# Agent attention with a maxout FFN: a new head, a new instruction order, and spare products to hold the clock

One Trainium2 chip (trn2), one core. The metric is the device time of that core in microseconds (us). It is 1.7 to 2.1 us longer than the span of the same execution (474.81 to 472.9 in the profile of the kernel before). Engines: PE is TensorE (matrix products), DVE VectorE, ACT ScalarE, POOL GpSimd, SPq the queue that issues most DMA transfers. The *granted clock* is the share of full speed at which TensorE was allowed to run.

## The reference

```python
B, N, C = 4, 12544, 128              # 49 agents, d_ff 768
def sm(a, b):
    e = exp(scale * (a @ b.T) - max);  return e / e.sum(-1)
agent_v = sm(agents, k) @ v          # per batch 49x128
x       = sm(q, agents) @ agent_v    # 50176 rows in all
h       = maximum(maximum(x @ w1, x @ w2), x @ w3)
out     = h @ w_out
```

## The kernel before

Batch 0's `k` and `v` (11 pairs of loads of up to 9x128 rows) are reduced to `agent_v` in a *head*, ahead of everything else. Then come 49 *groups* of 1024 q rows. Three times a batch ends inside a group (12, 24, 36); the k and v of the next batch are reduced in 11 of the 12 groups ahead of it, one pair each. So there are *groups with k* (33) and *without*.

The weights are folded into the small matrix: `G` holds `agent_v` times (w3 - w1), (w2 - w1) and w1 w_out. In a group, for each of six column blocks f: product **u** (PE), relu **a** (ACT), product **v** (PE), maximum **x** (DVE); block 4 is done wholly on ACT. Then 48 output products of 128x128 per group, `oc<o><f>` in 12 pieces of four, and a scaling `sc` by the softmax sums (DVE).

```python
def uv_tile():    ... tag="uv", bufs=3      # PSUM, two banks each
def small_tile(): ... tag="om", bufs=2      # PSUM, one bank each
def first(f):      uv[f] = hidden(f, C31, True)        # "u", 49-row products in pairs
def relu_first(f): ... nc.scalar.activation(a_sb[f], u, AF.Relu)           # "a"
def second(f):     uv[f] = hidden(f, C21, f != FI)     # "v"
def max_second(f): ... nc.vector.tensor_tensor(out=r, in0=uv[f], in1=a_sb[f], op=ALU.max)  # "x"
# [...]
def add_exps():   # POOL: Eacc += e_k       def reduce(): # DVE: e_sum = sum of Eacc over j
def total():      # PE, fp32: ones x e_sum  def normalise(): # DVE: avT = Vacc / total
# [...]  the program order is a table of keys; a group adds 6.0 per step, all is sorted by key
KEY = {"qt": -6.429, "qe": -5.981, "s": -0.613, "ex": -0.611, "u0": 0.67, "a0": 0.672, "ho": 0.873,
       "ks": 0.877, "sum": 0.878, "ke": 0.992, "u5": 1.063, "v0": 1.099, ... }
```

qt, qe, s, ex are the q transposes, their copy, the scores and `e_q`; ks, ke, kv, ka the scores of a k tile, `e_k`, the value products and the addition to Vacc; sum and rec the softmax sums and their reciprocals (`recips`). The engines execute in order what the table says.

The softmax here doesn't subtract the row's maximum and nothing guards it: scores larger than these inputs give would overflow.

## Time and profile before

| | before |
|---|---|
| time, median of 4 fast runs | 475.25 us (474.17 to 475.29) |
| span, granted clock (mean) | 472.9 us, 0.968 |
| first hidden product | 54.33 us |
| from one `e_q` to the next, with k / without | 8.17 / 7.96 us |

Three stages are read from the start of `e_q`, of which there is one per group. The prediction shows most lines. Here are the span and the chain of what ended last, from the page; the rows of the maxima and of the output products; and, from the timeline, the reduction ahead of a batch change, which matters later.

```profile
span 472.9 us, 13244 instructions
PE 72%; DVE 12%; DMA 10%; issue 2%; ACT 2%; POOL 0%; SPq 0%; DVEq 0%; ACTq 0%
L385 DVE TENSOR_TENSOR r<-uv_ps,a_sb 128x1024 bf16<-128x1024 f32 x245 | 298.2, 1223 | 6.9 <-PE uv_ps L360 4.4
```
```profile
140.48 0.94 POOL L209 TENSOR_TENSOR Eacc<-Eacc,e_k 128x392 f32<-128x392 f32 x1 [6.09 <-ACT e_k L193]
...
146.51 0.95 DVE L242 TENSOR_REDUCE e_sum<-Eacc 128x49 f32<-128x441 f32 x1
```

In the second fence POOL's last addition ends 5 us before DVE reduces (140.48 + 0.94 against 146.51): DVE never waits there before the change.

### The profile page before, as it was taken

The numbers are of one execution on the slowest core, as the hardware profiler recorded it, in microseconds if no ns is written. First come the engines' busy times: TensorE is split into PE (matmuls) and PEld (weight loads), VectorE is DVE, ScalarE is ACT, GpSimd is POOL, SyncE is SP. The second block draws the span as 40 slices with busy tenths as digits, with TensorE's granted clock in tenths as the row PEclk, the third lists the DMA queues.
The fourth block names the chain that finished last, engine by engine and source line by source line (L and its number), as shares of the span: only waits on it lengthen the run. The fifth ranks groups of instructions, "written<-read, shape, count | busy, mean of one in ns | idle before, by whom it ended". The sixth has DMA issues, their size and how long they took to land.

```text
span 472.9 us, 13244 instructions
## 1 busy us (share of the span) xinstructions
PE 433.8 (92%) x5434; PEld 281.7 (60%) x5434; DVE 417.2 (88%) x531; ACT 400.9 (85%) x455; POOL 177.4 (38%) x176
## 2 busy tenths in 40 slices
PE   2465699999999999999998999999999999999996
PEld 2454246666665666666665766666655666666654
DVE  3353479999999899999999899999999999999994
ACT  3364479999998899999997999999988898989982
POOL 2577643645524346363550544546130101010000
PEclk9996559999999999999999999999999999999999
DMA  8999998999998799998989799986524334341112
GB/s 319 403 411 409 346 318 259 289 323 231 289 312 268 238 285 342 310 292 219 299 300 292 257 297 277 342 260 161 157 90 137 132 134 137 128 141 76 60 69 114
DMA packets 67816, 114.93 MB, mean 243 GB/s; under 512 B 41831, under 2 KB 43307, under 8 KB 67755
## 3 DMA queue, kind: packets, MB, share of 16 engines
q1 hardware_dynamic: 67552, 113.98, 76.4%
q8 instruction: 42, 0.69, 0.6%
q14 instruction: 19, 0.16, 0.1%
q10 hardware_dynamic: 203, 0.10, 0.1%
HBM read 78.74 MB, written 25.69 MB: 221 GB/s over the span
## 4 chain that ended last, share of the span: by engine, by line
PE 72%; DVE 12%; DMA 10%; issue 2%; ACT 2%; POOL 0%; SPq 0%; DVEq 0%; ACTq 0%
PE uv_ps L360 29%; PE o_ps L399 27%; DVE r L385 9%; PE o_ps L390 5%; DMA st<-in_k_dram 5%; PE m_ps L324 4%; PE m_ps L334 3%; DMA st<-in_q_dram 2%; DMA kT<-k_bf 2%; DVE o_sb L406 2%; PE m_ps L188 2%; PE m_ps L197 2%; DMA st<-in_v_dram 1%; ACT a_sb L375 1%; PE m_ps L348 1%
## 5 line engine op out<-in xcount | busy, mean ns | idle before, releaser
L385 DVE TENSOR_TENSOR r<-uv_ps,a_sb 128x1024 bf16<-128x1024 f32 x245 | 298.2, 1223 | 6.9 <-PE uv_ps L360 4.4
L375 ACT ACTIVATE a_sb<-uv_ps 128x1024 bf16<-128x1024 f32 x245 | 241.0, 1025 | 23.0 <-PE uv_ps L360 22.9
L399 PE MATMUL o_ps<-wo_bf,r 128*128 128x128 bf16 x2352 | 200.2, 220 | 0.0
L360 PE MATMUL uv_ps<-e_q,G 49*128 49x512 bf16 (+3 forms) x1248 | 182.4, 376 | 3.4 <-ACT a_sb L375 1.6
L399 PEld LDWEIGHTS <-r 128*128 128x128 bf16 x2352 | 142.6, 98 | 60.8 <-issue 58.2
L360 PEld LDWEIGHTS <-G 49*128 49x128 bf16 x1248 | 58.9, 94 | 69.3 <-issue 25.4
L209 POOL TENSOR_TENSOR Eacc<-Eacc,e_k 128x441 f32<-128x441 f32 (+1 forms) x40 | 41.4, 1036 | 131.9 <-ACT e_k L193 107.5
L319 POOL CAST q_bf<-st 128x1024 bf16<-128x1024 f32 x49 | 51.0, 1042 | 71.1 <-DMA st<-in_q_dram 56.2
L406 DVE TENSOR_TENSOR o_sb<-o_ps,recips 128x512 f32<-128x512 f32 x98 | 67.2, 685 | 1.8 <-PE o_ps L399 1.8
L162 POOL CAST k_bf<-st 128x1152 bf16<-128x1152 f32 (+1 forms) x44 | 50.6, 1150 | 15.8 <-DMA st<-in_k_dram 15.0
L372 ACT ACTIVATE uv_ps<-uv_ps 128x1024 f32<-128x1024 f32 x49 | 49.4, 1008 | 1.7 <-PE uv_ps L360 1.4
L383 ACT ACTIVATE r<-uv_ps 128x1024 bf16<-128x1024 f32 x49 | 49.9, 1018 | 0.0
L390 PE MATMUL o_ps<-G,e_q 128*128 128x256 bf16 x196 | 38.1, 276 | 0.0
L169 POOL CAST v_bf<-st 128x1152 bf16<-128x1152 f32 (+1 forms) x33 | 37.6, 1140 | 0.0
L328 DVE COPY qT<-m_ps 128x1024 bf16<-128x1024 bf16 x49 | 33.4, 681 | 0.6 <-PE m_ps L324 0.6
L340 ACT ACTIVATE e_q<-m_ps 128x512 bf16<-128x512 f32 x49 | 29.3, 597 | 4.6 <-PE m_ps L334 4.1
L324 PE MATMUL m_ps<-ident,q_bf 128*128 128x128 bf16 x392 | 31.2, 225 | 1.6 <-POOL q_bf L319 1.6
L167 ACT ACTIVATE v_bf<-st 128x1152 bf16<-128x1152 f32 (+1 forms) x11 | 12.7, 1151 | 16.4 <-DMA st<-in_v_dram 16.4
L324 PEld LDWEIGHTS <-q_bf 128*128 128x128 bf16 x392 | 24.8, 100 | 2.8 <-POOL q_bf L319 2.1
L176 PE MATMUL uv_ps<-ident,k_bf 128*128 128x128 bf16 x98 | 11.2, 289 | 15.9 <-POOL k_bf L162 13.3
L182 DVE COPY kT<-uv_ps 128x1152 bf16<-128x1152 bf16 (+1 forms) x11 | 8.3, 750 | 19.8 <-PE uv_ps L176 19.8
L334 PE MATMUL m_ps<-qT,agT 128*64 128x512 bf16 (+3 forms) x104 | 20.6, 402 | 0.4 <-DVE qT L328 0.4
(60 smaller groups left out, 203.7 us busy)
## 6 DMA issues: line engine op xcount, KB each, us to landing
st<-in_q_dram SPq DMA_DIRECT2D x46, 512.0 KB, 5.0
out_dram<-o_sb SPq DMA_DIRECT2D x46, 512.0 KB, 3.2
st<-in_k_dram SPq DMA_DIRECT2D x40, 576.0 KB, 6.1
st<-in_v_dram SPq DMA_DIRECT2D x40, 576.0 KB, 7.1
st<-in_k_dram SPq DMA_DIRECT2D x4, 512.0 KB, 6.5
st<-in_v_dram SPq DMA_DIRECT2D x4, 512.0 KB, 7.0
wst<-in_moe_w_dram SPq DMA_DIRECT2D x3, 384.0 KB, 8.1
st<-in_q_dram SPq DMA_DIRECT2D x2, 384.0 KB, 4.2
```

The costliest lines, as they stand in the source:

```text
L162: nc.gpsimd.tensor_copy(out=d["kb"][:, :n, :], in_=d["k"][:, :n, :])
L209: nc.gpsimd.tensor_tensor(out=Eacc[b][:, :n * A], in0=Eacc[b][:, :n * A], in1=d["e"][:, :n * A], op=ALU.add)
L319: nc.gpsimd.tensor_copy(out=d["qb"], in_=d["q"])
L324: nc.tensor.transpose(t[:, j * P:(j + 1) * P], d["qb"][:, j, :], ident)
L360: nc.tensor.matmul(t[:, h, j0 * P:j1 * P], G[b][h * H:h * H + A, col + f * P:col + (f + 1) * P], d["e"][h * H:h * H + A, j0 * P:j1 * P], s ...
L372: nc.scalar.activation(u, u, AF.Relu)
L375: nc.scalar.activation(a_sb[f], u, AF.Relu)
L383: nc.scalar.activation(r, uv[f], AF.Relu)
L385: nc.vector.tensor_tensor(out=r, in0=uv[f], in1=a_sb[f], op=ALU.max)
L390: nc.tensor.matmul(t[:, i * 2 * C:(i + 1) * 2 * C], d["e"][:, jj * P:(jj + 1) * P], G[batch[jj]][:, C1O:C1O + 2 * C], start=(i == 0), stop ...
L399: nc.tensor.matmul(t[:, c:c + C], r_sb[f][:, h, jj * P:(jj + 1) * P], wo_bf[:, f, :], start=False, stop=True, skip_group_check=True)
L406: nc.vector.tensor_tensor(out=d["out"][:, j:j + m, :], in0=d["o", o].rearrange("p (j c) -> p j c", c=C), in1=d["r"][:, j:j + m].unsqueeze( ...
```

## The change

Its intent: end the head as soon as the loads allow, run the first groups at full clock, and take waits out of the steady group. The diff, cut to its core:

```diff
-    KEY = {"qt": -6.429, ..., "s": -0.613, ..., "rec": 1.248, ..., "kv": 1.624, ..., "x5": 4.465, ...}
+    KEY = {"qt": -1.706, ..., "s": -1.072, ..., "kv": 0.6, "ka": 0.601, "u0": 0.67, "rec": 0.684,
+           "a0": 1.809, "u2": 1.974, "v0": 2.084, "x0": 2.085, ..., "v5": 6.666, "x5": 6.771, ...}
+    WARM = 4
+    TAIL = (0.0005, 1.0, 1.5)
 # head: k loads lead v by three; sums on PE; values add up in one PSUM tile
+        def totals(d, g):   # replaces Eacc on POOL, reduce on DVE, fp32 sum on PE
+            for j in range(d["n"]):
+                nc.tensor.matmul(acc["t"][:, :A], ones_bf, d["e"][:, j * A:(j + 1) * A], ...)
+        def cast_v(d, g):   # last two: half on ACT, half on DVE
+        def product(c0, c1):
+            nc.vector.tensor_copy(out=G[0][:, c0:m], in_=src[:, :m - c0])
+            nc.scalar.activation(G[0][:, m:c1], src[:, m - c0:c1 - c0], AF.Copy)
+            if g >= 2:
+                at(c + 3.95, lambda: warm(WARM))        # spare products, ident x ident, 512 columns
+        at(z + 3.95, normalise)
+        at(z + 3.955, differences_21)                   # w2 - w1, w3 - w2: DVE and POOL
 # batches 1 to 3: hosts one group later, loads streamed, G one group ahead of the border
+    STREAM = {"kl": 0.0, "ld": 0.5, "kc": 1.0, "qc": 1.5, "vl": 1.9, "kt": 2.0, "vc": 3.2}
-            s = None if b == 0 else (b - 1) * NT // GT + g
+            s = (b - 1) * NT // GT + g + 1
+        z = 6.0 * (s - 1)
+        k_tail(b, s - 1, (z - 6 + KEY["ke"] + 1.6, z + KEY["kv"] + 0.0005,
+                          z + KEY["ka"] + TAIL[0], z + TAIL[1], z + TAIL[2]))
 # weight work after the head, spare output-like products in groups 0 and 1
+    at(HEAD_END + 0.5, cast_w1)
+    at(5.0, turn_w1)
+    at(7.0, prep_linear)
+    at(z, lambda ...: keep_busy((s, o), f))             # where the pieces of groups -2, -1 would stand
```

## The prediction

> **What bounds the kernel now.** I read the page first (busy shares, then the slices), then the timeline where the slices change, then the chain and the waits. The first fence is the page's share line and three of its slice rows (a slice is 11.8 us).
>
> ```profile
> PE 433.8 (92%) x5434; PEld 281.7 (60%) x5434; DVE 417.2 (88%) x531; ACT 400.9 (85%) x455; POOL 177.4 (38%) x176
> PE   2465699999999999999998999999999999999996
> DVE  3353479999999899999999899999999999999994
> PEclk9996559999999999999999999999999999999999
> ```
>
> PE, DVE and ACT are all near full from slice 6 on, so 400 us run well; the first five or six slices do not, and the clock falls to half in slices 3 to 5. There are three stages.
>
> *Head, 0 to 54.3 us.* Batch 0's k and v must be reduced before the first output group can start. The stretches and then the timeline show it:
>
> ```profile
> 30.00:40.00 10.00, 5.83 (x114) 5.40 (x111) 3.59 (x8) 5.88 (x9) 7.23 (x7) 0.98 1.02 409
> 40.00:50.00 10.00, 5.71 (x70) 4.81 (x71) 3.11 (x7) 2.69 (x4) 8.48 (x10) 0.50 1.02 412
> 60.00:65.00 5.00, 4.65 (x35) 2.07 (x35) 4.06 (x5) 4.10 (x5) 0.23 (x1) 0.50 0.97 356
> 80.00:90.00 10.00, 10.00 (x131) 6.58 (x130) 9.80 (x14) 9.66 (x12) 4.19 (x4) 1.00 0.93 301
> ```
> ```profile
> 40.30 1.06 ACT L167 ACTIVATE v_bf<-st 128x1024 bf16<-128x1024 f32 x1 [0.94 <-DMA st<-in_v_dram]
> ...
> 47.85 0.93 POOL L209 TENSOR_TENSOR Eacc<-Eacc,e_k 128x392 f32<-128x392 f32 x1
> 48.81 0.95 DVE L242 TENSOR_REDUCE e_sum<-Eacc 128x49 f32<-128x441 f32 x1 [4.17 <-POOL Eacc L209]
> ...
> 51.06 1.03 DVE L254 TENSOR_TENSOR avT<-Vacc,k_recip 128x49 bf16<-128x49 f32 x1
> 52.15 1.71 PE L266 MATMUL uv_ps<-wall,avT 128*64 128x512 bf16 x10 [1.67 <-DVE avT L254]
> ...
> 54.33 0.60 PE L360 MATMUL uv_ps<-e_q,G 49*128 49x512 bf16 x2 [0.48 <-ACT G L273]
> ```
>
> In the stretches the last two columns are DMA share and GB/s, and before them the granted clock. The DMA runs at 410 GB/s until 50 us, but the last v of batch 0 is there at 40.3 us; 14.0 us pass until the first hidden product (L360). They go into exponent sums added on POOL behind casts for later groups (done at 48.8), a reduce, a sum over partitions, a reciprocal, a normalise, the G products and their copies.
>
> *Groups 0 to 3.* The PE works, but at half clock until 70 us. The starts of e_q, one per group, are 45.25, 59.23, 69.20, 77.88, 86.05.
>
> *Steady groups and batch changes.* Here e_q is 8.17 us apart, and 7.96 us in the last twelve groups, which carry no k and v work. At each batch change the intervals are 8.12, 9.33 and about 10.1, together 3.1 us more than three steady ones.
>
> ```profile
> 288.41 0.60 ACT L340 ACTIVATE e_q<-m_ps 128x512 bf16<-128x512 f32 x1
> 296.58 0.60 ACT L340 ACTIVATE e_q<-m_ps 128x512 bf16<-128x512 f32 x1
> ```
> ```profile
> DVE recips L354 <- ACT e_k L193: 1.2, 6, 0.2
> ```
>
> The wait (of the stretch 90 to 140 us) recurs in every group: DVE stands 0.20 us before the reciprocal, plus some tenths in the gaps that count as busy. From start to start DVE needs 1.14 to 1.17 for each of five maxima, 0.60 to 0.64 for each scaling, 0.63 for the q copy, 0.12 and 0.14 for the small ones: 7.9 us of the 8.17. So DVE bounds a steady group.
>
> **What the Trainium skill says.** (1) "TensorE: Matmul & The Clock Gate", Part 1: the array starts at half clock, and about 3.4 us of sustained activity release it. The trace agrees on the factor: eight 128-column transposes take 1.03 us at 42.77 and 0.61 at 289.07. It agrees less on the trigger: PE counts as busy without a gap from 65 us on and is still at 0.50. The clock comes at about 70.3 us, some 2.6 us after the first 128x128 output products (L399, 67.96). Before 32.8 us the page's 1.0 is no measurement: nine transposes took 1.14 us at 6.76. (2) The same page, Part 4: transposes do not count as PE activity in the same way. That fits: in the head PE mostly transposes, got the full clock only about 32.4 us and lost it at 39.6. So both kinds of spare product (full-array 512-column ones in the head, 128-column output-like ones in groups 0 and 1) aim at what the trace shows missing. (3) "SBUF — State Buffer", Who interferes with whom: a VectorE instruction with two SBUF inputs contends with a GpSimd instruction that reads SBUF. The trace agrees: L254 took 1.03 us under a POOL cast and 0.22 in other batches. (4) "Perfetto Trace Analysis", Roofline: one core is bounded by its 16 DMA engines at about 435 GB/s; the trace shows 412, so I count 410.
>
> **The change part by part.**
>
> *Load order and reduction in the head.* What must land is 12.85 MB of k and v, 1.18 MB of w1 to w3, 0.52 MB of q and 0.1 MB of agents: 14.65 MB. Before moved 307, 396 and 411 GB/s in the first three tens of us, 11.14 MB; the remaining 3.51 MB at 410 take 8.6 us: landed at 38.6 us, with v slightly before w2, the last. What then follows, from rows of before: half a v cast on each of ACT and DVE 0.6 (1.06 for the whole), eight value products 0.55, normalise 0.25 (it now reads PSUM, so no lock), differences on DVE 0.7 for 512 columns (1.47 for 768, partly locked by POOL), G products 0.5, half a copy 0.5 (0.95 for 768 columns). Some lie side by side; with hops of 0.05 and some POOL contention I choose 2.9 us. First hidden product at 41.5 in place of 54.33: **12.8 us saved**. Gone from this path are the Eacc additions, reduce, fp32 sum and the wait for POOL. Four spare products of 512 columns are 0.9 us at full clock in a period of 2.9 us per k/v pair, beside the loads.
>
> *Groups 0 to 3 at full clock.* From the first hidden product to e_q of group 4 it is 31.7 us before. After: 5.3 to e_q of group 1, then 7.8, 7.8 and 7.95, plus 0.8 for the weight work moved here (cast 0.83, copy 0.56, two small evacuations) and 1.5 for a start-up wait (rival b): 31.2. **0.5 us saved**, the clock gain mostly eaten by the other two.
>
> *New order in a group.* The built order on DVE is max, max, scale, max, add V, reciprocal, max, scale, max, q copy: the reciprocal now follows the add, which already waited for e_k, so the 0.20 wait is gone. Against it stands the chain max, release of its PSUM buffer, product, max: 1.22 + 0.05 + 0.50 (the wait seen at 454.05 to 454.55) = 1.77, against 1.14 + 0.60 to 0.64 of DVE work between; it just fits. Sum: 1.165 + 1.78 + 1.14 + 0.12 + 0.15 + 1.78 + 1.14 + 0.63 = 7.9; I take 7.93 with k and v and 7.82 without. From e_q of group 4 to that of 48 there are 44 intervals, 30 of the first kind, 14 of the second: 347.4 us.
>
> *Batch changes.* The G products now come one group early, not at the border, but their ACT copy (1.02) stands ahead of a relu that a maximum needs, and DVE still has reduce 0.6, reciprocal and normalise 0.55 and the copy 0.86. I count 2.6 us each in place of 3.1. So 347.4 + 7.8 = 355.2 against 366.3 before: **11.1 us saved**.
>
> *End.* From e_q of group 48 to the end it is 20.5 us; e_q now stands about 1 us nearer to its first product: 19.5.
>
> **Sum:** 41.5 + 31.2 + 355.2 + 19.5 = 447.4 us of span, against 472.9. The time is 2.3 us over the span (475.2 to 472.9): 449.8. As several chains fit only by hundredths I add 1.2: **451 us**.
>
> **Rivals.** (a) *The steady order gains nothing.* PE issues strictly in order, about 7.3 us of products in 7.9, and the loop max to q copy to max to relus is nearly as long as DVE's work. If it stays at 8.17 and 7.96, the end is 10 us later: 461. For it: PE is 99% busy now; against: that busy is modelled overlap and the removed wait is DVE's own. (b) *The gain of the head becomes a wait for loads.* Before had moved some 4 MB more by its first hidden product; after starts with little in hand, and each kT transpose waits for its k and holds the SP queue (6.12 us of SPq at 44.73; it landed after 10.3). The first scores need kT about 47; I see it at 46, and the v cast of that group after w_out's at 48 to 50. That is 0 to 5 us; 1.5 are in the sum, the worst gives 455. Against more: with k and v a group needs 2.2 MB, at 340 GB/s (65 to 75 us) 6.5 us. (c) *The spare products do not hold the clock*: groups 0 and 1 run cold with 24 more products of 0.107 us each: 6 us more, 457. (d) *Better than I think*: no start-up wait, batch changes hidden: 445.
>
> **Range and chances.** The head's gain rests on bytes and a short chain (12 to 14 us nearly sure, 2.7%), so less than 2% needs two rivals together. Range 445 to 461. Faster by over 2% 0.95, within 2% 0.045, slower 0.005.
>
> **What would show it.** First hidden product at 41 to 43 us. Granted clock 1.0 by 35 us and at 45 to 60. e_q at 7.9 to 8.0 us in groups with k and 7.8 without, no reciprocal waiting for e_k. At a batch change 2 to 3 us over three steady intervals. PE waiting for kT or v_bf between 45 and 60 us under 3 us. If e_q stays at 8.17 the third step is wrong; if the first hidden product is after 45, the first.

## The result, and the profile after

**470.96 us** (median of 470.1, 471.15, 470.78 and a run of 479.04 that is classed slow, for its time: its clock was 0.986, that of the fast ones 0.987 to 0.993) against 475.25. The ratio of the fast runs is 0.9909, 95% interval [0.9887, 0.9931]: within 2%, where 451 had been predicted. (A ratio here is the mean time of one kernel's fast runs over that of the other's of the same rounds, so not quite the ratio of the medians quoted.) The profiled run is a fast one.

The page's first lines, rows of its slices (11.7 us each) and its chain:

```profile
span 468.3 us, 13594 instructions
...
PE 437.8 (93%) x5622; PEld 284.1 (61%) x5622; DVE 416.3 (89%) x522; ACT 397.6 (85%) x456; POOL 169.0 (36%) x164
...
PE   2786799999999999999989999999989999999996
...
PEclk9998899999999999999999999999999999999999
...
PE 76%; DMA 9%; DVE 5%; issue 4%; ACT 3%; POOL 2%; SPq 1%; POOLq 0%; DVEq 0%; ACTq 0%
```

The half-clock slices are nearly gone and the fill-up of PE is sooner; the chain has less DVE (5 for 12%) and more PE. In the steady part PE's row has two slices with an 8 (20 and 29 from zero, at 234 and 339 us), both at a batch change; before had one.

| stage (us of span) | before | predicted | after | short of the prediction |
|---|---|---|---|---|
| to the first hidden product | 54.33 | 41.5 | 45.39 | 3.9 |
| from there to `e_q` of group 4 | 31.7 | 31.2 | 34.0 | 2.8 |
| `e_q` of group 4 to 48 | 366.3 | 355.2 | 369.1 | 13.9 |
| from there to the end | 20.5 | 19.5 | 19.8 | 0.3 |
| span | 472.9 | 447.4 | 468.3 | 20.9 |

So the head gained 8.9 us, and the first groups and the steady stage gave 2.3 and 2.8 back. Two thirds of the miss lie in the steady stage. Its pace, from the timeline (a group with k, then one without):

```profile
282.11 0.60 ACT L473 ACTIVATE e_q<-m_ps 128x512 bf16<-128x512 f32 x1
290.26 0.60 ACT L473 ACTIVATE e_q<-m_ps 128x512 bf16<-128x512 f32 x1
...
399.96 0.60 ACT L473 ACTIVATE e_q<-m_ps 128x512 bf16<-128x512 f32 x1
408.05 0.60 ACT L473 ACTIVATE e_q<-m_ps 128x512 bf16<-128x512 f32 x1
```

That is 8.15 us (before 8.17, predicted 7.93) and 8.09 us (before 7.96, predicted 7.82): groups without k became *slower*. The 13.9 us are made of 30 intervals x 0.22 = 6.6, 14 x 0.27 = 3.8, three batch changes with 10.7 us over steady intervals in place of 7.8 = 2.9, and 0.6 in single longer intervals.

The head's end, from the timeline:

```profile
39.59 0.63 ACT L216 ACTIVATE v_bf<-st 128x512 bf16<-128x512 f32 x1 [1.99 <-DMA st<-in_v_dram]
...
40.55 1.00 POOL L135 TENSOR_TENSOR wall<-wst,wst 128x384 bf16<-128x384 f32 x1 [1.22 <-DMA wst<-in_moe_w_dram]
...
43.20 1.59 DVE L135 TENSOR_TENSOR wall<-wst,wst 128x128 bf16<-128x128 f32 x2
...
45.39 0.39 PE L493 MATMUL uv_ps<-e_q,G 49*128 49x512 bf16 x2
```

The last v is there at 39.6 us and w2 at 40.5 (predicted 38.6 for the last), and 4.9 us follow where 2.9 were predicted; DVE's differences take 1.59 where 0.7 was put in.

The first groups, as stretches (us, then busy time of PE, PEld, DVE, ACT, POOL with counts in brackets, granted clock, DMA share, GB/s) and as timeline:

```profile
50.00:55.00 5.00, 3.00 (x39) 1.83 (x39) 2.89 (x4) 3.70 (x6) 4.12 (x5) 1.00 0.88 231
55.00:60.00 5.00, 4.95 (x41) 2.48 (x41) 2.68 (x4) 2.31 (x4) 2.06 (x2) 0.66 0.81 318
```
```profile
51.50 0.49 PE L156 MATMUL m_ps<-ident,w_bf 128*128 128x128 bf16 x6 [0.59 <-ACT e_q L473]
...
52.04 0.56 DVE L157 COPY w1T<-m_ps 128x768 bf16<-128x768 bf16 x1 [1.96 <-PE m_ps L156]
```

Here the w1 transposes (L156), which the change put into group 1, wait for a PSUM buffer that `e_q` sets free, and DVE stands 1.96 us for them. PE is busy for 3.0 of 5 us, and the clock drops in the next stretch. `e_q` of group 2 comes 12.2 us after that of group 1.

And the group ahead of a batch change:

```profile
233.20 1.04 POOL L325 CAST v_bf<-st 128x1024 bf16<-128x1024 f32 x1 [1.95 <-DMA st<-in_v_dram]
234.20 1.02 POOL L349 TENSOR_TENSOR Eacc<-Eacc,e_k 128x441 f32<-128x441 f32 x1
...
235.25 0.96 DVE L382 TENSOR_REDUCE e_sum<-Eacc 128x49 f32<-128x441 f32 x1 [0.24 <-POOL Eacc L349]
```

POOL's addition, which ended 5 us ahead of the reduction before, now ends at the very moment at which DVE wants it: it stands behind a v cast, and that behind a load.

### The profile page after: what moved, and what is told of

The parts are those of the page before. It is cut to its first block, busy times and chain, and to the rows that moved or that the text cites. A ratio compares the mean times of both kernels' runs of the same rounds, so it can differ in the third digit from the quotient of the medians.

```text
span 468.3 us, 13594 instructions
## 1 busy us (share of the span) xinstructions
PE 437.8 (93%) x5622; PEld 284.1 (61%) x5622; DVE 416.3 (89%) x522; ACT 397.6 (85%) x456; POOL 169.0 (36%) x164
## 3 DMA queue, kind: packets, MB, share of 16 engines
q1 hardware_dynamic: 67552, 113.98, 77.2%
## 4 chain that ended last, share of the span: by engine, by line
PE 76%; DMA 9%; DVE 5%; issue 4%; ACT 3%; POOL 2%; SPq 1%; POOLq 0%; DVEq 0%; ACTq 0%
PE uv_ps L493 29%; PE o_ps L532 27%; DMA st<-in_k_dram 7%; PE o_ps L523 5%; PE m_ps L457 4%; PE m_ps L467 3%; DVE r L518 3%; PE m_ps L337 2%; ACT a_sb L508 2%; DMA st<-in_q_dram 1%; PE m_ps L187 1%; POOL q_bf L452 1%; PE m_ps L481 1%; DVE qT L461 1%; PE uv_ps L312 0%
## 5 line engine op out<-in xcount | busy, mean ns | idle before, releaser
L532 PE MATMUL o_ps<-wo_bf,r 128*128 128x128 bf16 x2352 | 172.3, 220 | 0.0
L532 PEld LDWEIGHTS <-r 128*128 128x128 bf16 x2352 | 139.7, 98 | 40.0 <-issue 37.6
L493 PEld LDWEIGHTS <-G 49*128 49x128 bf16 x1248 | 55.4, 94 | 67.4 <-issue 34.1
L321 POOL CAST k_bf<-st 128x1152 bf16<-128x1152 f32 (+1 forms) x33 | 37.4, 1134 | 41.0 <-DMA st<-in_k_dram 41.0
L349 POOL TENSOR_TENSOR Eacc<-Eacc,e_k 128x441 f32<-128x441 f32 x27 | 27.6, 1024 | 3.8 <-ACT e_k L192 3.8
L523 PEld LDWEIGHTS <-e_q 128*128 128x128 bf16 x196 | 12.1, 96 | 25.5 <-issue 25.5
L216 ACT ACTIVATE v_bf<-st 128x1152 bf16<-128x1152 f32 (+1 forms) x11 | 11.7, 1063 | 10.6 <-DMA st<-in_v_dram 10.6
```

Of the source, the lines that this page charges most:

```text
L493: nc.tensor.matmul(t[:, h, j0 * P:j1 * P], G[b][h * H:h * H + A, col + f * P:col + (f + 1) * P], d["e"][h * H:h * H + A, j0 * P:j1 * P], s ...
L523: nc.tensor.matmul(t[:, i * 2 * C:(i + 1) * 2 * C], d["e"][:, jj * P:(jj + 1) * P], G[batch[jj]][:, C1O:C1O + 2 * C], start=(i == 0), stop ...
L532: nc.tensor.matmul(t[:, c:c + C], r_sb[f][:, h, jj * P:(jj + 1) * P], wo_bf[:, f, :], start=False, stop=True, skip_group_check=True)
```

## The experiments

The recorded texts use letters. **D**: DVE's own work sets the steady pace (my prediction). **P**: PE is simply full. **L**, **K**: closed loops of products, maxima and PSUM buffers set the pace of groups without k (L) and with k (K). **T**: copies of G at a batch change. **W**: the weight work in group 1 stalls the start. **Q**: the spare products in PE's queue delay the head's end. **R**: the reduction waits for POOL and a load.

The times of after, p_prep5, r_late, r_only and r_tail are medians of 4 to 6 runs; the others are looks of one run. Looks of one run have no state of their own; from these I use spacings that repeat many times in the trace, and say so where it is otherwise. All measured values:

| label | result | us | before, same chip | first hidden | `e_q` 4 | with k | without k | first, second long interval at the changes |
|---|---|---|---|---|---|---|---|---|
| after | right | 470.96 | 475.25 | 45.39 | 79.41 | 8.15 | 8.09 | 8.80 10.83, 9.04 10.84, 9.21 10.84 |
| s_scale | wrong | 474.12 | 475.64 | 45.77 | 79.86 | 8.15 | 8.09 | 8.80 10.71, 12.39 11.33, 10.08 10.71 |
| s_piece | wrong | 473.56 | 475.64 | 45.78 | 80.84 | 8.15 | 8.09 | 9.50 10.61, 10.44 11.74, 8.93 10.61 |
| s_both | wrong | 472.51 | 475.64 | 46.52 | 80.81 | 8.15 | 8.09 | 9.32 10.49, 9.45 10.50, 9.93 11.96 |
| t_split | right | 473.18 | 475.64 | 45.92 | 81.27 | 8.15 | 8.09 | 8.72 11.35, 10.54 10.64, 8.72 10.64 |
| s_loop | wrong | 466.98 | 475.72 | 45.52 | 79.54 | 8.15 | 7.91 | 9.30 10.61, 8.67 10.89, 9.48 10.61 |
| o_v0first | right | 481.31 | 475.72 | 45.87 | 81.44 | 8.28 | 8.08 | 9.06 10.80, 11.49 12.07, 9.77 12.21 |
| p_prep | right | 466.72 | 475.72 | 46.82 | 76.44 | 8.15 | 8.09 | 8.71 10.83, 9.22 10.84, 9.33 10.84 |
| h_warm | right | 473.69 | 475.72 | 46.23 | 82.40 | 8.15 | 8.09 | 9.62 10.83, 8.71 11.07, 8.72 10.83 |
| d_chain | wrong | 473.04 | 475.72 | 46.88 | 80.51 | 8.09 | 8.09 | 9.51 10.83, 8.89 10.84, 10.97 11.94 |
| d_two | wrong | 462.97 | 475.72 | 45.15 | 78.05 | 8.09 | 7.91 | 8.81 10.61, 8.64 10.70, 8.83 10.61 |
| k_kv | right | 490.48 | 475.72 | 45.85 | 81.97 | 8.80 | 8.09 | 9.42 10.97, 9.43 10.84, 9.43 10.84 |
| h_diff | right | 477.40 | 475.72 | 45.86 | 80.35 | 8.15 | 8.09 | 13.59 12.54, 9.31 10.84, 8.72 10.83 |
| c_nospare | right | 475.18 | 475.73 | 46.90 | 81.23 | 8.15 | 8.09 | 11.26 12.22, 8.71 10.84, 8.98 10.84 |
| c_nowarm | right | 473.34 | 475.73 | 45.57 | 81.74 | 8.15 | 8.09 | 9.57 10.84, 8.71 10.84, 9.63 10.84 |
| p_prep5 | right | 470.44 | 475.73 | 45.98 | 75.60 | 8.15 | 8.09 | 8.71 11.02, 11.54 13.71, 10.79 12.19 |
| r_late | right | 464.96 | 475.73 | 47.58 | 77.20 | 8.15 | 8.09 | 8.15 11.09 in all three |
| r_only | right | 468.78 | 475.95 | 45.92 | 79.82 | 8.15 | 8.09 | 8.15 11.44, 8.15 11.10, 8.15 11.10 |
| r_tail | right | 463.58 | 475.95 | 46.39 | 76.01 | 8.15 | 8.09 | 8.15 11.15, 8.15 11.30, 8.15 10.62 |

### Is it DVE? Is it PE? (s_scale, s_piece, s_both)

```diff
# s_scale: half of each group's second scaling left out on DVE (POOL writes zeros there)
+            h = m // 2 if o else m
+            if h < m: nc.gpsimd.memset(d["out"][:, j + h:j + m, :], 0.0)
-  out=d["out"][:, j:j + m, :], ...   +  out=d["out"][:, j:j + h, :], ...
# s_piece: an output piece left out on PE         # s_both: both
+            if (o, f) == (0, 2): return
```

> Wrong result on purpose: the second scaling of each group takes half its columns on DVE (GpSimd zeroes the rest), so DVE has about 0.3 us less work per group. Theory P (PE is full in a group with k and v: products plus the array's change between 49-row pairs and full-array products; a chain maximum, buffer, product, four output pieces, second scaling sets the groups without k): e_q interval with k stays 8.10 to 8.15 us, without k falls from 8.09 to 7.8-7.9. Theory D (DVE sets both, as I predicted): both fall by 0.3 us, to about 7.85 and 7.8.

> Wrong result on purpose: four of the 48 output products of a group (the piece of f=2 in the first half) are left out, 0.22 us of PE, at a place that is not in the chain to the second scaling. Theory P: interval with k falls from 8.15 to about 8.09, where the chain binds; without k unchanged at 8.09. Theory D: unchanged in both.

> Both of these cuts at once. Theory P: with k 7.9 to 7.95 us (PE less 0.22 us), without k 7.8-7.9. Theory D: the same as the DVE cut alone, about 7.85 with k.

From the timelines of s_both (`e_q`, a group with k, then one without) and of s_scale (the halved scaling and the maximum behind it):

```profile
283.46 0.60 ACT L473 ACTIVATE e_q<-m_ps 128x512 bf16<-128x512 f32 x1
291.61 0.60 ACT L473 ACTIVATE e_q<-m_ps 128x512 bf16<-128x512 f32 x1
...
402.80 0.60 ACT L473 ACTIVATE e_q<-m_ps 128x512 bf16<-128x512 f32 x1
410.89 0.60 ACT L473 ACTIVATE e_q<-m_ps 128x512 bf16<-128x512 f32 x1
```
```profile
282.76 0.42 DVE L542 TENSOR_TENSOR o_sb<-o_ps,recips 128x256 f32<-128x256 f32 x1
283.37 1.22 DVE L518 TENSOR_TENSOR r<-uv_ps,a_sb 128x1024 bf16<-128x1024 f32 x1 [0.19 <-PE uv_ps L493]
```

The halved scaling took 424 ns in place of 681, so DVE was spared 0.26 us per group, and PE 0.22; neither alone nor both together moved 8.15 or 8.09 by as much as 0.01. **D falls** for the changed order, and with it the main step of my prediction: DVE nearly fills its 8.15 us, but what it is spared becomes a wait (0.19 us for a product of PE, in the second fence). No run took work out of the kernel before, so what set its 8.17 is not shown. P, as a plain sum, falls too: without (0,2) PE waits 0.22 us later on for the buffer of x0. Nothing is concluded from the times of these single runs (their batch changes differ, see R).

### A loop in the groups without k (s_loop, o_v0first)

In a group without k the timeline closes this loop: x1 ends, its PSUM buffer goes to u0, 16 output products stand behind it in PE's order, then u2 and v0; x0, the copy of qT, x2, x3 follow on DVE; x3 frees the buffer of v1; x1. If so, a piece among the 16 counts in full and the piece (0,2) not at all.

```diff
# s_loop                                # o_v0first
+  if (o, f) == (1, 0): return          -  "v0": 2.084,   +  "v0": 1.9735,     # ahead of u2
```

> Wrong result on purpose: the output piece f=0 of the second half is left out, four products or 0.22 us of PE, this time between u0 and v0 in PE's order. The two cuts before changed no interval, so theories P and D have fallen as sole bounds. New theory L: the interval is one chain through all three engines: maximum x1 frees a PSUM buffer, u0, sixteen output products, u2, v0, maximum x0, q copy, maxima x2 and x3, v1, x1 again (0.05+0.32+1.00+0.23+0.49+1.14+0.64+1.22+1.77+1.22 = 8.08 us by the trace). Then without k 8.09 falls to 7.87-7.92, with k 8.15 to 7.93-8.0. Rival (some other chain): unchanged, as for the two cuts before.

> Right result: v0 stands before u2 in PE's order, nothing else changed. Theory L: u2's 0.23 us leave the chain, so e_q intervals of about 7.9-7.95 us without k and 7.95-8.1 with k (there the next chain through e_k is near). Rival: unchanged 8.09 and 8.15.

s_loop took the groups without k from 8.09 to 7.91 and left those with k at 8.15. The same amount of PE work as in s_piece, elsewhere: **L holds** for the groups without k. The `e_q` of s_loop, from its timeline:

```profile
398.55 0.60 ACT L473 ACTIVATE e_q<-m_ps 128x512 bf16<-128x512 f32 x1
...
406.46 0.60 ACT L473 ACTIVATE e_q<-m_ps 128x512 bf16<-128x512 f32 x1
```

o_v0first is no way out: v0 ahead of u2 left them at 8.08 and made groups with k slower (8.28). The new order is one in which several loops are almost equally long, and moving one piece lengthens another.

### The groups with k (d_chain, d_two, k_kv)

```diff
# d_chain                               # d_two
+  if (o, f) == (0, 4): return          +  if (o, f) in ((0, 4), (1, 0)): return
# k_kv: value products and their addition behind v5, u0 and x5
+            if s + 1 not in tails: keys.update(kv=0.6705, ka=0.78)
```

> Drops the output-like piece (0,4) of every group (four 128x128 products, about 0.23 us of PE, result wrong on purpose). It stands on PE between the product of the maximum x1 and that of the maximum x5. Theory K (in a group with k and v two stretches close a loop: PE without a gap from the product freed by x0 to the product of x5, about 4.83 us, then x5, its buffer, v0, x0, its buffer, about 3.32 us): unlike the pieces (0,2) and (1,0) dropped before, this one lies in the PE stretch, so groups with k fall from 8.15 to between 7.93 and 8.02 us (DVE's own work stops it from the full 0.23), groups without k stay at 8.09. Rival (the interval is fixed by something outside these stretches, such as loads or the e_k chain): 8.15 stays, as in the other two.

> Drops (0,4) and (1,0), one piece in each stretch (result wrong on purpose). Theory K: groups with k 7.92 to 7.98, groups without k 7.91 as with (1,0) alone; span about 8 to 9 us under the changed kernel. Rival: groups with k stay at 8.15 and only those without move, span about 3 us under.

> Moves the nine value products and the addition of V behind the products v5 and u0 and the maximum x5, in all groups with k but those before a batch change (result right). Theory K with a full PE (the products and the changes of shape add up to 8.15, and both stretches are equally long): PE's sum is unchanged, groups with k stay at 8.15 (8.12 to 8.25). Rival (the wait of the value products for e_k sets the loop): 8.15 falls to about 7.95, span 5 us less.

(0,4) is the first piece that moved the groups with k at all, but by 0.06 (8.09), not by 0.13 to 0.22; with (1,0) left out as well they stay at 8.09, while those without k go to 7.91 again. So **K holds in kind and fails in size**. In d_chain PE now waits 0.17 us in its longest run of hidden products, for the buffer of x3. A third loop (x0, qT, x2, x3, products, value products, four more output products, v5, x5, v0, x0) would give that, but no run took a piece out of it: what sets 8.09 is open. k_kv missed both of its expectations (8.80): `recips` reads the same PSUM tile that the value products write, so the reciprocal, and x5 behind it, waited for the moved products.

What PE does need can be read from the starts of its single instructions in the kernel after: one pair of hidden products follows another after 0.22 us, but another kind of product follows the last pair only after 0.31; an output product follows another after 0.056, but a hidden pair follows after 0.151. So a run of 49-row products costs about 0.095 us on entering and 0.09 on leaving. A group with k has five such runs, and the q scores, which stand ahead of one of them, cost another 0.115: about 1.0 us by these starts. My 7.3 us of products had left it out; with it PE's products follow one another through the 8.15 us of a group with k without a gap.

### Batch changes (t_split, r_late, r_only, r_tail)

```diff
# t_split: each G copy half DVE, half ACT, behind a0
-    TAIL = (0.0005, 1.0, 1.5)      +    TAIL = (0.0005, 1.85, 1.9)
+            nc.vector.tensor_copy(out=G[b][:, c0:c0 + m], in_=src[:, :m])
+            nc.scalar.activation(G[b][:, c0 + m:c1], src[:, m:], AF.Copy)
# r_only: the reduction behind x0, the q copy, x2 and x3
-        k_tail(b, s - 1, (z - 6 + KEY["ke"] + 1.6, ...
+        k_tail(b, s - 1, (z + 0.3, ...
# r_late: r_only and p_prep together     # r_tail: r_late, and TAIL = (0.0005, 1.85, 1.9)
```

> At a batch change both G copies are split between DVE and ACT and stand after the relu a0 in ACT's order, right result. Theory T (ACT's in-order G copy ahead of a relu, while its products wait, is what makes the long interval): the long e_q interval (10.84 us) falls to 9.8-10.2, the whole cost of a change over steady groups from 3.3-3.8 us to 2.4-2.9. Rival (the added work of DVE, reduce, reciprocal and copies, sets it): 10.7 or more remains.

t_split took the second long interval from 10.84 to 10.64 in two of three places, to 11.35 in one: the two halves write one tile and ran one after the other. T explains little.

What stood out were the *first* long intervals: 8.6 to 13.6 us between runs whose code there was the same. In h_diff, the worst:

```profile
137.39 1.04 POOL L325 CAST v_bf<-st 128x1024 bf16<-128x1024 f32 x1 [1.34 <-DMA st<-in_v_dram]
138.39 1.02 POOL L349 TENSOR_TENSOR Eacc<-Eacc,e_k 128x441 f32<-128x441 f32 x1
139.45 0.94 DVE L382 TENSOR_REDUCE e_sum<-Eacc 128x49 f32<-128x441 f32 x1 [4.58 <-POOL Eacc L349]
```

DVE stands 4.58 us for an addition on POOL that is not long itself, but is in order behind casts whose loads came late (1.34 us for this v; the k cast ahead of it, at 133.70, had stood 3.54 us for its own). PE then runs dry, and the clock falls to 0.51 in the stretch 140 to 145. Over the 16 profiles with this order the wait ranged from none to 4.6 us.

> The weight work moved into the head (as before, which gave 466.7 us) and, new, the reduction of the exponent sums at a batch change placed 4 us later in DVE's order, behind two maxima (result right). Theory R (in the group before a batch change DVE stands for POOL's last addition, which stands behind a v cast that waits for its load; 0.1 to 4.6 us in the runs so far, so the first long interval is 8.6 to 13.6): no wait before the reduction, the first long intervals all 8.6 to 8.8, the second 10.6 to 11.0, time 464 to 466 us, about 1 us under the kernel with the weight work moved alone. Rival (the late loads hold PE or ACT as well): the interval keeps values of 9 or more.

> The same kernel as the one with the weight work moved into the head, timed in rounds. 466 to 468 us, 1.6 to 2.0% under the kernel before; its time scatters by 1 to 4 us with the wait before the reduction.

> The changed kernel with the late reduction alone (weight work where the change put it; result right). Theory R: long intervals 8.15 and 11.1 at every batch change, no wait before the reduction, time 468 to 470 us with a scatter under 2 us, mostly from the start-up; the kernel as changed gave 470.1 to 479.0. Rival: the scatter of the changed kernel comes from elsewhere and stays, with times of 471 to 475.

In r_late the load is as late as ever, but nobody waits (its timeline):

```profile
129.72 1.04 POOL L325 CAST v_bf<-st 128x1024 bf16<-128x1024 f32 x1 [3.20 <-DMA st<-in_v_dram]
130.73 1.02 POOL L349 TENSOR_TENSOR Eacc<-Eacc,e_k 128x441 f32<-128x441 f32 x1
...
135.79 0.94 DVE L382 TENSOR_REDUCE e_sum<-Eacc 128x49 f32<-128x441 f32 x1
```

The first long interval is 8.15, an ordinary one, at all nine changes of r_late, r_only and r_tail, so **R holds**. In rounds: r_late 464.96 us (464.48 to 465.56), ratio 0.9775 [0.9762, 0.9787]; p_prep5, the same without the move, 470.44 (468.99 to 474.58), 0.9895 [0.9863, 0.9928]. One changed key is worth 1.2% and takes away nearly all of the scatter. (The run of 479.04 of the change may be that scatter too; no trace of it was kept.) Sizes were missed: the first interval came out below the expected 8.6 to 8.8, the second (11.09) above 10.6 to 11.0, and p_prep5 (470.44) above 466 to 468, where p_prep's single look had been 466.72. r_only, the change with this one key moved, is 468.78 (468.44 to 469.15), 0.9852 [0.9833, 0.9870].

> The kernel with the weight work in the head and the late reduction, and at a batch change ACT's copy of G behind the relu a0 in place of ahead of it; the order on PE and DVE is the same (result right). Theory T (in the second long interval ACT stands 2.0 us before that copy, with a relu ready behind it, and DVE's maximum x0 waits 0.6 to 0.7 us for the relu): the second long interval falls from 11.09 to 10.2 to 10.6, span 1.5 to 2.7 us less, time about 463. Rival (the group products on PE and the G copy itself set it, because u2 and v0 need G): 11.0 to 11.4 stays.

On ACT the wait before the G copy fell from 2.27 to between 0.54 and 0.63 us, and the second long interval stayed in two places of three: 11.15, 11.30, 10.62. So ACT's order is not most of what it is made of (its rival, PE's group products and the copies themselves, is left, not shown). The expected time of about 463 us was met by luck, for the interval that it rested on did not fall. r_tail is still the fastest right kernel: 463.58 us (462.67 to 464.06), 0.9742 [0.9724, 0.9759]. Its lead over r_late comes from other rounds; in the two profiles 1.2 of 1.4 us lie ahead of `e_q` of group 4, where the code is the same.

### The start (p_prep, h_warm, h_diff, c_nospare, c_nowarm)

```diff
# p_prep: w1 cast and transposes in the head        # h_diff: differences ahead of the last values
-    at(HEAD_END + 0.5, cast_w1)                    -  at(z + 3.955, differences_21)
+    at(in_head(15.6), cast_w1)                     +  at(z + 3.35, differences_21)
-    at(5.0, turn_w1)
+    at(in_head(15.9), turn_w1)                     # c_nowarm: no spare products in the head
# h_warm: none after the last two k/v pairs         -            if g >= 2:
+            if 2 <= g < last - 1:                  +            if False:
# c_nospare: no spare products in groups 0 and 1
-                if z > HEAD_END:   +                if False and z > HEAD_END:
```

> Right result: the cast and the transposes of w1 stand in the head and not in group 0. Theory W (the copy of the transposed w1 stands in DVE's order before two maxima and waits for a PSUM buffer that e_q of group 1 frees, PE idles, the clock drops for 3.4 us): the interval from e_q of group 1 to that of group 2 falls from 12.2 to 8.5-10 us, and the clock stays full from 50 to 60 us. Rival S (the supply of kT and v after the early start): stays above 11.5 us.

The stretches of p_prep that answer to those of the kernel after:

```profile
50.00:55.00 5.00, 4.59 (x57) 2.42 (x55) 4.41 (x7) 4.95 (x7) 3.98 (x5) 1.00 0.80 267
55.00:60.00 5.00, 4.67 (x54) 2.85 (x53) 3.68 (x4) 4.26 (x7) 2.40 (x3) 1.00 0.97 335
```

PE is busy for 4.6 us of 5 and keeps the clock; `e_q` of group 2 follows after 8.8 us, not 12.2, again in p_prep5, r_late and r_tail. **W holds**: `e_q` of group 4 comes at 75.6 to 77.2 us in these four, at 78.1 to 81.3 in the nine other runs that keep the start of the change and are not slower in pace.

> Right result: no spare products after the last two k/v pairs of the head. Theory Q (they stand in PE's in-order queue ahead of the last value products and of the G products, at half clock): the first hidden product comes at 43.5-44.7 us in place of 45.4-45.9. Rival (the landing of v and w2 and the differences under POOL's lock set it): 45 us or later. If the spares did hold the clock, groups 0 and 1 get longer, e_q of group 0 to group 2 over 20.5 us.

> Emits the second set of weight differences ahead of the last value products and the normalisation, so that DVE does them while it waits for the values (result right). Theory (the head's end is set by DVE's differences, 1.59 us under POOL's lock, which hold up the first G copy): first hidden product at 44.3 to 44.9 in place of 45.4. Rival (the loads and the spare products ahead of the last values set it): stays at 45.3 to 45.8.

> The changed kernel without the spare output-like products in groups 0 and 1 (result right). If they hold the clock there, it falls to about half until 60 to 70 us and e_q of group 4 comes 2 to 5 us later than the 78 to 82 us of the runs so far; if the real products and the spare ones of the head hold it, e_q of group 4 comes at 78 to 81, or a little sooner, for 24 products of 0.06 to 0.1 us are gone.

> The changed kernel without any spare products in the head (result right). PE then mostly transposes there: granted clock 0.5 from somewhere before 40 us until about 60 to 66, as without those of the last two pairs, e_q of group 4 at 82 to 86 us; the first hidden product at 45.5 to 47, because DVE and the loads set it.

Without the spare products of the last two pairs the first hidden product is not sooner (46.23), so Q falls as the only cause; instead the clock is gone for 15 us. From the stretches of h_warm:

```profile
45.00:50.00 5.00, 4.32 (x28) 1.90 (x29) 2.53 (x5) 3.56 (x6) 0.16 (x1) 0.50 0.88 251
50.00:55.00 5.00, 4.85 (x30) 2.14 (x28) 1.50 (x4) 2.51 (x3) 3.83 (x4) 0.50 0.87 256
```

h_diff missed too (45.86): the normalisation was done at 43.4, but the four spare products ahead of the G products ran at half clock until 44.7. Both obstacles stand side by side, and taking away one leaves the other; no run took away both. The runs with an unchanged head scatter from 45.15 to 46.90 anyway, so a test of half a microsecond here needs more than one look. Without any spare products in the head, `e_q` of group 4 is at 81.7 us and the clock at 0.50 from 40 to 60; without those in groups 0 and 1 it is at 81.2 and the clock at 0.50 from 50 to 60. The nine unchanged starts have 80.0 on average. But c_nospare's head, which is unchanged, happened to end late (46.90). Counted from each run's own first hidden product, `e_q` of group 4 follows after 34.3 us in c_nospare, after 36.2 in c_nowarm and h_warm, and after 32.9 to 35.4 (34.1 on average) in those nine. So the spare products of the head are worth some 2 us, in two looks; for those in groups 0 and 1 no gain in time is shown.

## Why the prediction was wrong, step by step

**Head.** The mechanism was right (sums off POOL, no wait behind casts), the size was not: 8.9 us of 12.8, where 12 to 14 were called nearly sure; by its own sign (a first hidden product after 45 us) this step was wrong too. The loads ended at 40.5, not 38.6; the rest took 4.9 us, not 2.9. The biggest mis-sized term is the differences, 1.59 us for 0.7, beside POOL's q cast (0.75 in h_diff, where they ran earlier). That spare products at half clock stood in PE's queue as well I had counted only "beside the loads".

**Groups 0 to 3.** Put at 31.2, measured 34.0. I had allowed 0.8 us for the weight work and 1.5 for a start-up wait that I expected at kT. PE waited for neither kT nor v_bf between 45 and 60 us, so rival (b) did not come. The wait came at the weight work's own PSUM buffer and cost 3.4 us of one interval with the clock it lost (W, shown by four runs). Rival (c), that the spare products do not hold the clock, is half true: those of the head are worth some 2 us, those of groups 0 and 1 (32, not 24) did not hold it through that stall (0.66 from 55 to 60 us) and show no gain.

**New order in a group.** This step failed: "So DVE bounds a steady group" and the 7.93 and 7.82 built on it. s_scale shows that in the new order less DVE work buys nothing: 8.15 and 8.09 stay. What sets them is a closed loop through PE, DVE and PSUM buffers: shown by s_loop for groups without k; for those with k d_chain shows only that PE's stretch has a part in it, and the rest stays open. My check of PE, "about 7.3 us of products", left out about 1.0 us for changing between 49-row pairs and full-array products; the Trainium skill has a sentence on that, in "TensorEngine Tiling (Array Packing)", Key Properties (a change of the tiling mode drains the array), which I had not looked up, and this case's 0.31 for 0.22 and 0.151 for 0.056 us agree with it. The chain that I did write down, maximum, buffer, product, maximum, "just fits" only if PE is free at that instant, and it is not. Rival (a) is what happened, and worse: groups without k lost 0.13 us each to loop L.

**Batch changes.** Put at 2.6 us over steady intervals each, measured 3.3 to 3.8 in the profiled run, up to 9.8 in others, and 2.9 in r_late, without the wait. I had counted 0.6 us for the reduction (it takes 0.95) but not what it waits for, since before it waited for nothing. The change moved POOL's addition behind a v cast and the reduction close behind the addition (R, shown). Why the loads come late at times is open.

**End, and the sum.** The end was right within 0.3 us. The four stages are all off in the same direction, so the range of 445 to 461, made for the rivals one at a time, did not hold. "Less than 2% needs two rivals together" was wrong: of the rivals only (a) came in full, and the rest of the miss (the head's 3.9 us, the stall at the weight work, the reduction's wait) was in none of them. Two small slips: the 2.3 us from span to time compare two executions (1.9 within one), and the clock before came 2.4 us, not 2.6, after the first output products (70.3 less 67.96).

## What to carry to other kernels

When an engine looks full in a tuned loop, take work from it at *two* different places before believing that it sets the pace: the same 0.22 us of PE work was worth nothing at one place and 0.18 us at another. An instruction on an engine with little slack that needs a result from an in-order side engine inherits every wait in that engine's queue, loads included; placing it 4 us later lengthened the second interval by 0.25 us (10.84 to 11.09) and still gained 1.2% in all. And a prediction that adds durations has to add what lies between different kinds of products too.

## What the Trainium skill lacked or had wrong

- "TensorEngine Tiling (Array Packing)", Key Properties: it says that a change of tiling mode drains the array, but not what that costs. Here it is 0.09 us on leaving a run of 49-row pairs and about 0.095 on entering one, about 1.0 us of a group of 8.15 in all.
- "TensorE: Matmul & The Clock Gate", Part 1: the condition of some 3.4 us of sustained activity does not tell from the profile's busy share when the clock comes. In h_warm PE counts as busy for 4.32 and 4.85 us of two stretches of 5 us, at 0.50 throughout.
- "Perfetto Trace Analysis", Optimization Strategy, has only that a gap which keeps coming back can mean too few buffers. No page has the closed loop of PSUM buffers in which taking 0.26 us from DVE and 0.22 from PE per group changes the interval by less than 0.01 us (8.15 and 8.15).
